# One scheduler for a whole kernel: pooled and local attention feeding a gated MLP

## The chip, the cores and the metric

The kernel runs on one core of one Trainium2 chip. The metric is the device time of one execution in microseconds (us). It has five kinds of worker: TensorE (PE in the profile, its weight loads PEld), VectorE (DVE), ScalarE (ACT), GpSimd (POOL) and the DMA queue that SyncE feeds (SP).

## The reference, cut to what matters

```python
def _attn_ref(q, k, v):                       # (8, 8, 576, 64) each
    q_d, k_d, v_d = (a.reshape(B, H, 144, 4, D).mean(axis=3) for a in (q, k, v))
    out_up = np.repeat(sm_attn(q_d, k_d, v_d), 4, axis=2)      # softmax attention on means of 4
    mask = np.abs(pos[:, None] - pos[None, :]) < 4
    scores = np.where(mask, scale * q @ k.T, -1e9)             # 7 neighbours at most
    return out_up + softmax(scores) @ v

def _moe_ref(x, w_gate, w_val, w_out):        # x (4608, 512), 512 -> 1536 -> 512
    return (sigmoid(x @ w_gate) * (x @ w_val)) @ w_out
```

The output of the attention, laid out by token, is the x of the MLP. All is float32 at the outside.

## The kernel before, in words

**Work.** Attention is done in 32 units of two heads: unit u is batch u // 4. The MLP is done in 9 chunks of 512 tokens (a batch has 576), each with 12 slices of the hidden width: a gate product (`pg`), a value product (`pv`), and an output product (`po`) that adds up in four PSUM banks. Numbers that need more than 16 bits are carried as a high and a low float16 part, so a product is three matmuls, and each tile is split twice: a high part by ACT and a low part by DVE or POOL.

**Three stretches.** First, batches 0 and 1 (units 0 to 7, function `early`, line 966), the loading and splitting of the weights (`wload`, `wmant`, `wshift`, `wjoin`, `wmax`, `whigh`, `wlow`, lines 210 to 252) and chunk 0 of the MLP. Second, chunk 1, while `combos` (line 736) forms the sums and differences of weight blocks from which the other chunks work with seven block products instead of eight, and writes them to DRAM. Third, chunks 2 to 8 by `pair` (line 816; its products are the matmuls at line 799), with the attention of batches 2 to 7 (units 8 to 31, function `later`, line 460) beside them.

**Operations of a unit.** `s` and `sd` are the local and the pooled scores on PE; `st`, `mx`, `sm`, `rc`, `dm`, `rd` are mask, maxima, sums and reciprocals on DVE; `ex`, `de` the exponentials on ACT; `sb`, `tm` subtract the maximum and multiply by the reciprocal, on POOL in `later` (line 507), and `tm` on DVE for batch 0 and on POOL for batch 1 in `early` (`divide`, line 1023); `pa`, `pb` add four q and k columns to one (lines 990, 995, and 624, 486 in `later`), `va`, `vB` the same for v (lines 1087, 1092, and 624, 575), all on POOL; `dn` normalizes the pooled weights; `tt`, `dt` are transposes, `do` and `x0`, `x1` the two products with v on PE; `oc` copies `do` out with the scale of the batch; `xa` adds both and `xh`, `xl` split the result (`xlow`, line 1130, on POOL).

**The scale of a batch.** v is scaled by a power of two that comes from a bound of its size over the batch: `vm` (function `vmax`, line 315) sums absolute values of one unit on ACT, `vs` brings the four units to one number over PE and DVE. For batch 0 `vm` reads `vd`, the tile that the pooled v is made from; for batches 1 and up it reads a tile of its own that `vload` (line 309) fetches, 320 KB per unit. In `early`, `do` waits for `vs` of its batch.

**Who sets the order.** Every operation has a name, an engine, an estimated duration and a list of operations that it must follow. There are two lists and two planners. `op` and `order` (line 1254) plan the first stretch; `op2` and `arrange` (line 1433) plan the rest. Both go forward in time and give a free engine the ready operation with the earliest latest start; `GOALS` (line 22) holds due times of the first list; `in_turn` is a hand-made order of PE for the second. `arrange` starts each engine where its work in the first list ends:

```python
free = {g: max([end[k] for k in seq if ops[k]["eng"] == g and k[:2] != "st"] + [0.0]) for g in engs}
```

At the end both plans are merged by planned start, and the instructions are issued in that order, engine by engine (line 1530). An engine works through its own instructions in order; between engines there are semaphores where data require them, and no others. Neither planner has an idea of one engine slowing another. Where PE is planned to be idle before chunk 0, `awake` (line 85) puts in matmuls whose results nobody reads.

**Memory.** `arena` holds staging tiles of the weights first and x of chunks 2 and up later, so a marker named `arena` stands before the second use: it follows the stores of chunk 0, its last `pv` and the joining of the output weights.

Of the kernel before, what the change touches and what calls it, by code (L numbers as in the profile page):

```python
# [21 lines left out]
GOALS = {'x0': 23.22, 'x0s': 8.14, 'pv': 48, 'pvs': 7.76, 'x1': 105.9, 'x1s': 18.75, 'po': 139.42, 'pos': 2.17}  # L22
# [37 lines left out]
GSCALE = 2.0 ** -17  # L60
# [10 lines left out]
def attention_moe(ctx, tc, qk, qkd, v, vd, wg, wv, wo, mask, out):  # L71
# [28 lines left out]
    head = part(40960, 2048).rearrange("p (h t) -> p h t", h=NPAIR)  # L100
    turns = {}
# [187 lines left out]
    def ratios(got):  # L289
# [9 lines left out]
        nc.vector.tensor_scalar(out=qmax, in0=qmax, scalar1=e, scalar2=2.0 ** -11, op0=ALU.mult, op1=ALU.mult)  # L299
# [15 lines left out]
    def vmax(u):  # L315
# [3 lines left out]
        src = vdraw[u].rearrange("p a b f -> p (a b f)") if u < NPAIR else vraw[u].rearrange("p a b -> p (a b)")  # L319
# [134 lines left out]
    work = {}  # L454

    def op2(name, eng, us, f, after=(), att=()):
        assert name not in work, name
        work[name] = dict(name=name, eng=eng, us=us, f=f, after=[a for a in after if a is not None], att=att)

    def later(u):  # L460
# [7 lines left out]
        def was(k, back):  # L468
            return f"{k}_{u - back}" if u - back >= NPLAIN else None
# [4 lines left out]
        def add(k, eng, us, f, after=(), att=()):  # L474
            op2(n(k), eng, us, f, [n(a) if a[-1] != "!" else a[:-1] for a in after if a is not None], [n(a) for a in att])
# [149 lines left out]

        add("qk", "D", 2.2, lambda: load_qk(u), [old("s", 2)])
        add("qkd", "D", 2.1, lambda: load_qkd(u), [old("pb", 1)])
        add("vd", "D", 1.4, lambda: load_vd(u), [old("vB", 1)])
        add("vw", "D", 1.2, lambda: vload(u), [old("vl1", NVR), f"x1{5 if u % NVR in (2, 3) else 7}!" if u < NPLAIN + NVR else None, "vm7!"])
# [5 lines left out]
        add("s", "E", 0.9, scores, ["qk", old("tt1", 3)], ["st0", "st1"])  # L635
        for par in range(2):
            add(f"st{par}", "V", 0.55, lambda par=par: masked(par), ["s"])
        add("mx", "V", 0.95, lambda: reduce("mx", ALU.max), ["st0", "st1"])
        add("sb", "P", 1.55, lambda: each_group("mx", ALU.subtract), ["mx"])
        add("ex", "A", 0.84, lambda: nc.scalar.activation(s["t"], s["t"], AF.Exp), ["sb"])  # L640
        add("sm", "V", 0.95, lambda: reduce("sm", ALU.add), ["ex"])
# [11 lines left out]
        for par in range(2):  # L653
            add(f"tt{par}", "E", 0.37, lambda par=par: turn(par), ["tm"], [f"tl{par}"])
            add(f"tc{par}", "A", 0.4, lambda par=par: turned(par, 0), [f"tt{par}", old("x1", 2)])
# [23 lines left out]
    def xsfree(c):  # L679
        return [f"g_{(c - 3) * (NFC // 2) - 1}_1_3"] if c >= 4 else ["pv1_11"] if c == 3 else ["head"]  # L680
# [932 lines left out]
```

## Time and profile before

| | us |
|---|---|
| median of three runs | 1021.35 (1018.09 to 1021.99) |
| the profiled execution | 1022.47 |
| its span, first to last instruction | 1020.3 |
| PE busy in it | 983.4 (96%), granted clock 0.975 on the mean |
| DVE, ACT, POOL busy in it | 644.5, 581.6, 375.9 |

What lies around the span is 2.2 us. A busy PE counts matmuls whose ends are modelled and which overlap, and the `awake` matmuls too, so idle time of PE is a lower bound of what the stretch loses.

### The profile page before, as it was taken

What the parts mean: (1) busy time and instruction counts of PE and PEld (TensorE: products, weight loads), DVE (VectorE), ACT (ScalarE), POOL (GpSimd) and SP (SyncE); (2) the same over time, 40 slices, a digit from 0 to 9 for tenths busy, and PEclk for the clock granted to TensorE, in tenths of its full rate; (3) what the DMA queues carried; (4) which work ended last, traced back from release to release, by engine and by line L of the source; (5) the groups of instructions that cost most, each with busy time, mean ns of one, the idle gap of its engine ahead of it and who ended that gap; (6) DMA issues with size and microseconds to landing.
All of it is one profiled execution on the core that took longest, in us unless ns stands there. A gap on an engine that the chain in (4) does not pass through costs nothing.

```text
span 1020.3 us, 21707 instructions
## 1 busy us (share of the span) xinstructions
PE 983.4 (96%) x8776; PEld 684.9 (67%) x8776; DVE 644.5 (63%) x1113; ACT 581.6 (57%) x1453; POOL 375.9 (37%) x374
## 2 busy tenths in 40 slices
PE   6978999999998999999999999999999999999998
PEld 4853455544545777777777777777777777777775
DVE  5789988478999665656566657565765445233223
ACT  4667765555464765676657565756565645334333
POOL 6442222367776446344523453445243303000000
PEclk7679999999999999999999999999999999999999
DMA  9886576845544755565545554654453335434431
GB/s 318 281 281 232 206 247 213 281 170 180 175 148 150 252 188 185 184 206 207 185 161 207 208 190 155 217 207 167 155 189 110 111 110 183 143 111 138 157 109 42
DMA packets 57700, 187.72 MB, mean 184 GB/s; under 512 B 15616, under 2 KB 19200, under 8 KB 57600
## 3 DMA queue, kind: packets, MB, share of 16 engines
q1 hardware_dynamic: 57600, 186.34, 52.8%
q8 instruction: 69, 1.13, 0.4%
q14 instruction: 31, 0.25, 0.1%
HBM read 165.87 MB, written 20.45 MB: 183 GB/s over the span
## 4 chain that ended last, share of the span: by engine, by line
PE 78%; DVE 12%; DMA 5%; issue 2%; ACT 2%; POOL 1%; SPq 0%; DVEq 0%; POOLq 0%; ACTq 0%
PE bank L799 37%; PE po L420 25%; PE x L420 3%; PE pg L420 3%; DVE arena L753 2%; PE od L420 2%; DMA qk<-in_qk_dram 2%; PE pv L420 2%; PE s L425 2%; PE sd L425 1%; PE at L545 1%; DVE arena L759 1%; PE adt L565 1%; DMA qkd<-in_qkd_dram 1%; DVE g L921 1%
## 5 line engine op out<-in xcount | busy, mean ns | idle before, releaser
L420 PE MATMUL po<-g,wo 128*128 128x512 f16 x1188 | 313.3, 382 | 0.0
L799 PE MATMUL bank<-arena,wg 128*128 128x256 f16 x1764 | 220.1, 273 | 0.0
L799 PE MATMUL bank<-arena,wv 128*128 128x256 f16 x1764 | 220.1, 273 | 0.0
L799 PEld LDWEIGHTS <-wg 128*128 128x128 f16 x1764 | 171.2, 98 | 47.6 <-issue 1.0
L799 PEld LDWEIGHTS <-wv 128*128 128x128 f16 x1764 | 170.4, 98 | 47.8
L420 PEld LDWEIGHTS <-wo 128*128 128x128 f16 x1296 | 124.7, 98 | 86.7 <-issue 6.6
L921 DVE SCALAR_TENSOR_TENSOR g<-wg,g 128x512 f16<-128x512 f32 x84 | 78.4, 933 | 34.9 <-ACT g L917 34.2
L846 ACT COPY bank<-wv 128x256 f32<-128x256 f32 x84 | 31.6, 377 | 98.4 <-DVE wg L844 63.6
L844 DVE TENSOR_TENSOR wg<-bank,wv 128x512 f32<-128x512 f32 x63 | 43.2, 686 | 59.9 <-PE bank L799 59.8
L839 ACT COPY wv<-bank 128x512 f32<-128x512 f32 x84 | 49.0, 584 | 51.4 <-PE bank L799 49.7
L420 PE MATMUL pg<-arena,wg 128*128 128x512 f16 x288 | 70.6, 395 | 7.2 <-POOL arena L1136 3.3
L420 PE MATMUL pv<-arena,wv 128*128 128x512 f16 x288 | 67.0, 383 | 0.0
L917 ACT ACTIVATE g<-wg 128x512 f16<-128x512 f32 x84 | 52.8, 629 | 22.7 <-DVE wg L827 22.7
L618 DVE TENSOR_TENSOR arena<-x,od 128x112 f32<-128x112 f32 (+12 forms) x72 | 21.6, 349 | 59.4 <-PE x L420 59.2
L728 POOL TENSOR_TENSOR arena<-arena 128x512 f16<-128x512 f32 (+1 forms) x35 | 41.4, 1189 | 46.8 <-ACT arena L724 46.8
L597 DVE SCALAR_TENSOR_TENSOR vblk<-vring,svb,vblk 64x640 f16<-64x640 f32 x48 | 51.8, 1080 | 9.6 <-ACT vblk L595 8.5
L420 PEld LDWEIGHTS <-wg 128*128 128x128 f16 x288 | 28.0, 101 | 42.6 <-issue 8.4
L844 DVE TENSOR_TENSOR wv<-bank,wv 128x512 f32<-128x512 f32 x21 | 14.4, 687 | 60.2 <-PE bank L799 60.2
L420 PEld LDWEIGHTS <-wv 128*128 128x128 f16 x288 | 28.0, 99 | 32.1 <-issue 1.9
L624 POOL TENSOR_TENSOR qkd<-qkd 128x576 f32<-128x576 f32 x24 | 29.9, 1246 | 53.0 <-DMA qkd<-in_qkd_dram 53.0
L841 ACT COPY wv<-bank 128x256 f32<-128x256 f32 x84 | 31.0, 369 | 30.1 <-PE bank L799 28.3
L535 POOL TENSOR_TENSOR ad<-e,sme 72x288 f32<-72x288 f32 x48 | 35.2, 750 | 34.7 <-PE adt L565 25.7
(182 smaller groups left out, 1640.5 us busy)
## 6 DMA issues: line engine op xcount, KB each, us to landing
wg<-wg SPq DMA_DIRECT2D x42, 896.0 KB, 4.6
wv<-wv SPq DMA_DIRECT2D x42, 896.0 KB, 4.6
qk<-in_qk_dram SPq DMA_DIRECT2D x30, 610.0 KB, 6.1
qkd<-in_qkd_dram SPq DMA_DIRECT2D x29, 576.0 KB, 3.8
arena<-in_wo_dram SPq DMA_DIRECT2D x24, 512.0 KB, 4.8
vd<-in_vd_dram SPq DMA_DIRECT2D x29, 384.0 KB, 3.7
vring<-in_v_dram SPq DMA_DIRECT2D x28, 320.0 KB, 5.2
out_dram<-arena SPq DMA_DIRECT2D x16, 512.0 KB, 5.2
```

What stands on the lines that cost most here:

```text
L420: nc.tensor.matmul(o, w[a], x[c], start=first and i == 0, stop=last and i == len(pairs) - 1)
L425: nc.tensor.matmul(o, w, x, start=True, stop=True)
L535: nc.gpsimd.tensor_tensor(out=AD[:, qb].rearrange("p c h k -> p h c k")[:, :, :, :KC], in0=s["e"][:, qb].rearrange("p h (c k) -> p h c k", ...
L597: nc.vector.scalar_tensor_tensor(out=VB[ps, 1, :, ps], in0=src, scalar=sc, in1=VB[ps, 0, :, ps], op0=ALU.mult, op1=ALU.subtract)
L728: eng.tensor_tensor(out=lo, in0=src, in1=hi, op=ALU.subtract)
L799: nc.tensor.matmul(o, w[:, a, k], x[:, xb, k, c], start=start and z == 0, stop=z == len(mms) - 1, skip_group_check=True)
L839: op2(f"sa_{n}_{i}", "A", 0.58, lambda i=i: nc.scalar.copy(snap(i)[:, HC:], banks[i]), [g(0), p("ad"), p("se")] + (["w1"] if n == 0 else []))
L841: op2(f"sb_{n}_{i}", "A", 0.37, lambda i=i: nc.scalar.copy(snap(i)[:, :HC], banks[i][:, RIGHT]), [g(1)])
L844: lambda i=i: nc.vector.tensor_tensor(out=vsum(n) if i else duo(n)[:, 1], in0=banks[i], in1=snap(i)[:, :CH], op=ALU.add),
L846: op2(f"se_{n}_{i}", "A", 0.38, lambda i=i: nc.scalar.copy(banks[i][:, LEFT], snap(i)[:, CH:]), [f"ad_{n}_{i}"])
L917: nc.scalar.activation(g[:, 0], tanh[c, fc], AF.Copy, scale=GSCALE)
L921: nc.vector.scalar_tensor_tensor(out=g[:, 1], in0=t, scalar=GSCALE, in1=g[:, 0], op0=ALU.mult, op1=ALU.subtract)
```

## The change

1. `op2`, `work` and `arrange` are gone: all operations go into one list `ops`, planned by one `order`. An engine may take work of the second and third stretch as soon as it is ready. PE chooses, by earliest latest start, among the first list and the next 14 operations of `in_turn`, whose due times count from a new goal `c1`. Dependencies that followed from the break between the lists are written out (`SAME`, `was`).
2. The planner has a lock: while a POOL operation or a DVE operation of the kinds in `TWO` is planned, no other such operation starts.
3. Some operations of `early` may go to either engine, and the planner chooses: `pb` (now with `pa` in it) and `vB` (now with `va` in it) as one or two reductions on DVE or as the additions on POOL; `tm` and `xl` on either.
4. For batch 1, `vm` reads `vd`, and its four `vload` transfers are gone. `do` no longer waits for `vs`; for batch 1 `oc` copies without the scale, and a new small ACT operation `or` scales in place once `vs` is there.
5. Estimated durations and goals are changed (a qk load 2.1 for 1.49, a weight tile 1.7 for 1.28, latency of a DMA 2.6 for 2.2).
6. The tiles of tanh, of g and of x of one unit lie in one fixed tile `spare`; slots in the weights' memory are packed closer; a power of two is moved from one scale (`GSCALE`) to another.

The core of the diff:

```diff
-GOALS = {'x0': 23.22, 'x0s': 8.14, 'pv': 48, 'pvs': 7.76, 'x1': 105.9, 'x1s': 18.75, 'po': 139.42, 'pos': 2.17}
+GOALS = {'x0': 22.36, 'x0s': 7.49, 'pv': 73.39, 'pvs': 6.2, 'x1': 99.09, 'x1s': 19.72, 'po': 150.09, 'pos': 1.17, 'c1': 159.4}
...
-        src = vdraw[u].rearrange("p a b f -> p (a b f)") if u < NPAIR else vraw[u].rearrange("p a b -> p (a b)")
+        src = vdraw[u].rearrange("p a b f -> p (a b f)") if u < NPLAIN else vraw[u].rearrange("p a b -> p (a b)")
...
+        def prep():
...
+            if chosen[n("pb")] == "V":
+                nc.vector.tensor_reduce(flat_, x, axis=AX.X, op=ALU.add)
+                return
+            nc.gpsimd.tensor_tensor(out=x[:, :, 0:2], in0=x[:, :, 0:2], in1=x[:, :, 2:4], op=ALU.add)
+            nc.gpsimd.tensor_tensor(out=flat_, in0=x[:, :, 0], in1=x[:, :, 1], op=ALU.add)
...
+            if chosen[n("vB")] == "V":
+                for ps in HALVES:
+                    nc.vector.tensor_reduce(VDB[ps, :, ps], vdraw[u][ps], axis=AX.X, op=ALU.add)
+                return
...
-            nc.scalar.activation(s["od"], s["do"][:, :SD], AF.Copy, scale=sxb[:, b : b + 1])
+            nc.scalar.activation(s["od"], s["do"][:, :SD], AF.Copy, scale=sxb[:, b : b + 1] if first else 1.0)
+
+        def dscale():
+            nc.scalar.activation(s["od"], s["od"], AF.Copy, scale=sxb[:, b : b + 1])
...
-        unit_op("pa", "P", 1.3, prep_a, ["qkd"])
-        unit_op("pb", "P", 0.85, prep_b, ["pa"], new=[("qks", "qks_")], use=["qkd_"])
+        unit_op("pb", "V", 1.27, prep, ["qkd"], new=[("qks", "qks_")], use=["qkd_"], alt=("P", 2.1))
...
-        unit_op("tm", "V" if first else "P", 0.95 if first else 1.7, divide, ["rc"], use=["t_"])
+        unit_op("tm", "V", 0.95, divide, ["rc"], use=["t_"], alt=("P", 1.6))
...
-        unit_op("va", "P", 1.05, vda, ["vd"] + ["vm"] * first)
-        unit_op("vB", "P", 1.3, vdb, ["va"], new=[(f"vdb{u % 2}", "vdb_")], use=["vd_"])
-        unit_op("do", "E", 0.8, dout, ["dc", "vB", f"vs{b}!"], new=[("bank", "do_"), ("od", "od_")], use=["adt_", "vdb_"])
+        unit_op("vB", "V", 1.75, vdb, ["vd", "vm"], new=[(f"vdb{u % 2}", "vdb_")], use=["vd_"], alt=("P", 2.35))
+        unit_op("do", "E", 0.8, dout, ["dc", "vB"], new=[("bank", "do_"), ("od", "od_")], use=["adt_", "vdb_"])
...
-        unit_op("xl", "P", 1.6, xlow, ["xh"], use=["xs_"])
+        unit_op("xl", "P", 1.6, xlow, ["xh"], use=["xs_"], alt=("V", 0.85))
...
+    TWO = ("jn", "lo", "sh", "tm", "gl", "vl", "m", "p1", "p2", "cs", "cl", "t0", "t3", "t4", "t5", "t6", "t9", "ot", "ol", "a1", "xl")
+    two = lambda k, x: x == "P" or x == "V" and (k.startswith(TWO) and not k.startswith(("mx", "ml")) or k[:3] == "r1_")
...
+                for x in ENGS:
...
+                    for l, k in choices:
+                        if ops[k]["ways"][x][1] and port > now + 1e-9:
+                            continue
+                        got = places(ops[k], now) if ops[k]["new"] else []
+                        if got is not None:
+                            break
...
+                    if ops[k]["ways"][x][1]:
+                        port = end[k]
...
-    run = sorted([(start[k], i, k, ops[k]["f"]) for i, k in enumerate(seq)] + [(when[k], len(seq) + i, k, work[k]["f"]) for i, k in enumerate(turn_)])
     with tc.manual_schedule(engines={E.PE, E.DVE, E.Activation, E.Pool, E.SP}):
-        for _, _, k, f in run:
+        for k in seq:
             if k in spare:
                 awake(spare[k][1], spare[k][0])
-            f()
+            ops[k]["f"]()
```

`ENGS` is "NEVAPD": at one moment of the plan PE is asked first, then DVE, ACT, POOL, the DMA queue. The lock is a rule of the plan; the program that is issued has the same kinds of semaphores as before.

## Rows read from the trace of the kernel before

**Rows 1.** The page: span of the profiled execution.
```profile
span 1020.3 us, 21707 instructions
```

**Rows 2.** Windows: busy us of PE, PEld, DVE, ACT, POOL; PEclk, DMA share, GB/s.
```profile
0.00:17.00 17.00, 9.97 (x100) 6.61 (x100) 8.92 (x16) 8.40 (x21) 10.58 (x19) 0.90 0.91 317
17.00:66.00 49.00, 42.57 (x517) 36.38 (x517) 35.37 (x75) 30.32 (x96) 22.70 (x30) 0.69 0.94 295
66.00:125.00 59.00, 51.19 (x229) 22.78 (x229) 55.06 (x110) 43.17 (x102) 14.43 (x12) 0.91 0.63 221
125.00:198.00 73.00, 71.84 (x503) 41.73 (x503) 55.55 (x104) 41.80 (x93) 16.76 (x18) 1.00 0.71 245
198.00:334.00 136.00, 125.49 (x974) 66.12 (x972) 121.38 (x186) 72.58 (x177) 96.52 (x76) 0.97 0.49 170
334.00:860.00 526.00, 525.93 (x5307) 398.26 (x5306) 321.96 (x555) 325.87 (x845) 214.93 (x222) 1.00 0.51 180
860.00:1020.30 160.30, 156.40 (x1158) 112.98 (x1155) 46.21 (x69) 59.44 (x123) 0.00 (x0) 1.00 0.35 120
```

**Rows 3.** Windows of the awake matmuls alone: PE busy, PEclk, DMA share, GB/s.
```profile
17.00:66.00 49.00, 4.53 (x22) 0.69 0.94 295
```

**Rows 4.** Waits of PE from 17 to 66: us in total, times, longest.
```profile
PE s L1008 <- DMA qk<-in_qk_dram: 4.6, 2, 2.9
```

**Rows 5.** Waits of PE from 66 to 125.
```profile
PE pg L420 <- POOL arena L1136: 3.3, 1, 3.3
PE pg L420 <- ACT wg L248: 2.5, 2, 1.8
PE pg L420 <- DVE wg L252: 1.4, 2, 1.2
```

**Rows 6.** Waits of PE from 198 to 334, the two longest.
```profile
PE sd L425 <- DVE pvb L176: 2.1, 1, 2.1
PE mxt L165 <- DVE mxr L158: 1.9, 1, 1.9
```

**Rows 7.** DVE groups from 198 to 334: busy us, mean ns, idle before.
```profile
L753 DVE TENSOR_TENSOR arena<-arena 128x256 f32<-128x256 f32 x48 | 35.6, 781 | 1.9 <-POOL arena L748 1.3
L759 DVE TENSOR_TENSOR arena<-arena 128x1024 f16<-128x1024 f32 x12 | 18.8, 1563 | 0.4 <-ACT arena L756 0.3
L921 DVE SCALAR_TENSOR_TENSOR g<-tanh,g 128x512 f16<-128x512 f32 x12 | 14.0, 1165 | 1.2 <-ACT g L917 1.2
```

**Rows 8.** Timeline of DVE, two short instances: start us, us.
```profile
291.80 1.71 DVE L753 TENSOR_TENSOR arena<-arena 128x256 f32<-128x256 f32 x4
...
298.88 1.21 DVE L759 TENSOR_TENSOR arena<-arena 128x1024 f16<-128x1024 f32 x1
```

**Rows 9.** DVE groups from 860 to the end, where POOL is idle.
```profile
L921 DVE SCALAR_TENSOR_TENSOR g<-wg,g 128x512 f16<-128x512 f32 x22 | 15.2, 691 | 15.6 <-ACT g L917 15.6
```

**Rows 10.** Timeline of POOL, 214 to 222: start us, us.
```profile
214.94 1.47 POOL L507 TENSOR_TENSOR t<-t,sm 128x768 f32<-128x768 f32 x1
216.37 1.33 POOL L624 TENSOR_TENSOR qkd<-qkd 128x576 f32<-128x576 f32 x1
217.66 1.65 POOL L507 TENSOR_TENSOR t<-t,mx 128x768 f32<-128x768 f32 x1
219.27 1.00 POOL L624 TENSOR_TENSOR vd<-vd 128x384 f32<-128x384 f32 x1
```

**Rows 11.** Timeline of DVE in the same stretch.
```profile
215.02 5.54 DVE L753 TENSOR_TENSOR arena<-arena 128x256 f32<-128x256 f32 x4 [1.27 <-POOL arena L748]
```

**Rows 12.** POOL groups from 125 to 198: the lines of later.
```profile
L624 POOL TENSOR_TENSOR qkd<-qkd 128x576 f32<-128x576 f32 x1 | 1.2, 1151 | 0.0
L486 POOL TENSOR_TENSOR qks<-qkd 128x288 f32<-128x288 f32 x1 | 0.7, 712 | 0.1
```

**Rows 13.** DVE groups from 0 to 420: a reduction of 768 elements.
```profile
L504 DVE TENSOR_REDUCE mx<-t 128x12 f32<-128x768 f32 x9 | 8.5, 948 | 0.2
```

**Rows 14.** Timeline of PE: unit 4 transposed, scale of batch 1, its product.
```profile
97.15 0.59 PE L1079 MATMUL adt<-ident,ad 72*128 72x72 f32 x6
...
121.78 0.38 PE L266 MATMUL mxt<-ident,mxr 1*128 1x1 f32 x2
...
124.69 0.90 PE L420 MATMUL od<-adt,vdblk 128*128 128x144 f32 x6
```

**Rows 15.** The line of vload: issues by form, first and last start.
```profile
L311 SPq DMA_DIRECT2D vring<-in_v_dram x4: 327/328/422, 38.3 to 101.7; - x4
```

More of the change, by code (lines that the diff above doesn't have):

```diff
@@ L452, in pooled_pairs @@
                 for qb in range(2) for h in range(2)]
[L454 to L458, printed above, removed]
+    SAME = dict(s="s{}", pb="pb{}", sd="sd{}", vB="vB{}", tt0="tt0_{}", tt1="tt1_{}", dn1="dn{}", dt="dt{}", do="do{}", x1="x1{}", xa1="xa1{}", qk="qk{}", tc0="tc0_{}", oc="oc{}", mx="mx1_{}", sm="sm{}")
     def later(u):
@@ L474, in add @@
         def add(k, eng, us, f, after=(), att=()):
-            op2(n(k), eng, us, f, [n(a) if a[-1] != "!" else a[:-1] for a in after if a is not None], [n(a) for a in att])
+            op(n(k), eng, us, f, [n(a) if a[-1] != "!" else a[:-1] for a in after if a is not None], att=[n(a) for a in att])
         def old(k, back):
@@ L953, in attention_moe, with op, engine @@
     ops = {}
-    def op(name, eng, us, f, after=(), new=(), use=(), by=None):
+    freed = {}
+    def op(name, eng, us, f, after=(), new=(), use=(), att=(), alt=None):
         assert name not in ops, name
-        ops[name] = dict(name=name, eng=eng, us=us, f=f, after=list(after), new=list(new), use=list(use), by=by)
+        ops[name] = dict(name=name, eng=eng, us=us, f=f, after=[a for a in after if a is not None], new=list(new), use=list(use), alt=alt)
+        for z, x in enumerate(att):
+            ops[name]["new"].append((["att"], f"{name}.{z}"))
+            freed[f"{name}.{z}"] = x
+    chosen = {}
+    def engine(name):
+        return nc.vector if chosen[name] == "V" else nc.gpsimd
     where = {}
@@ L1023, in divide @@
         def divide():
-            eng = nc.vector if first else nc.gpsimd
-            eng.tensor_tensor(out=groups(), in0=groups(), in1=s["sm"].unsqueeze(2).to_broadcast([P, 4 * NH, WIN]), op=ALU.mult)
+            engine(n("tm")).tensor_tensor(out=groups(), in0=groups(), in1=s["sm"].unsqueeze(2).to_broadcast([P, 4 * NH, WIN]), op=ALU.mult)
         def turn(par):
@@ L1525, in attention_moe @@
-    turn_, when, fin = arrange()
+    CAPS = dict(qk=2, qkd=1, vd=1, vt0=1, vt1=1, vt2=1, vt3=1, qks=1, t=3, at=2, e=1, ad=1, adt=1, vdb0=1, vdb1=1, od=2, xs=1, stage=NST, wa=2,
+                tanh=2, g16=3, att=2, gate=1, val=1, o0=1, o1=1, o2=1, o3=1)
+    LAT = dict(D=2.6, E=0.3, V=0.12, A=0.12, P=0.15, N=0.0)
+    EXTRA, AHEAD = 0.5, 14
+    ENGS = "NEVAPD"
+    import heapq
+    after = {k: [] for k in ops}
+    users = {}
+    for o in ops.values():
+        o["after"] = list(dict.fromkeys(o["after"]))
+        for a in o["after"]:
+            after[a].append(o["name"])
+        for key in o["use"]:
+            users.setdefault(key, []).append(o["name"])
+        for _, key in o["new"]:
+            users.setdefault(key, []).append(o["name"])
+            if key in freed:
+                users[key].append(freed[key])
```

548 lines of the change are left out of this document (245 added, 303 removed).

## The prediction

> **What bounds the kernel now.** I read the page first and then cut the span into the kernel's own stretches [rows 1, 2]. From 334 us on PE is idle for 0.1 of 526 us and for 3.9 of the last 160.3 us: there TensorE is the bound, and no order of the other engines gives anything back. All that can be won lies before 334. The first 17 us are the start (PE idle 7.0). I call the next four stretches A (17 to 66, attention of batch 0), B (66 to 125, the first gate and value products), C (125 to 198, the rest of chunk 0 with batch 1) and D (198 to 334, chunk 1 with the weight combinations).
>
> In A PE is idle for 49 − 42.6 = 6.4 us, and another 4.5 us of its busy time are fillers [rows 3]; its granted clock is 0.69 on the mean, between the levels of 1.2 and 2.4 GHz, and the DMA engines are 94% busy: this stretch waits for loads, and the longest wait of PE is for a qk tile, 4.6 us [rows 4]. In B PE is idle for 7.8 us while DVE is busy for 55.1 of 59: the split weights come late (2.5 + 1.4 us), and once the low part of x from POOL does (3.3 us) [rows 5]. In C PE is idle for 1.2 us only; DVE is idle for 73 − 55.6 = 17.4 us and POOL for 56. In D PE is idle for 10.5 us, DVE is busy for 121.4 of 136 and POOL for 96.5; the longest waits of PE are for small DVE results that stood in DVE's queue behind longer work [rows 6].
>
> DVE in D is busier than its work. The difference of two weight blocks takes 781 ns on the mean and 1.71 / 4 = 0.43 us in a short instance; the low part of a combination takes 1563 ns against 1.21 us [rows 7, 8]; the low part of g takes 1165 ns against 691 where POOL is idle [rows 7, 9]. Where the two engines meet, four block differences take 5.54 us while four POOL instructions run back to back at 1.0 to 1.65 us each: DVE gets through about one per POOL instruction [rows 10, 11]. Over D that is 48 × 0.35 + 12 × 0.35 + 12 × 0.47 = 16.8 + 4.2 + 5.7 = 27 us of DVE's 121.
>
> **The change part by part.** Sums are made against the profiled execution, 1022.5 us; the median of the runs is 1.1 us less, and about 0.5% (5 us) is what a measurement of this kernel tells from no change.
>
> *One list.* The break between the lists keeps DVE and POOL from the attention of units 8 and up during C: POOL does one pooled q and k sum of such a unit there, nothing else of it [rows 12]. With one list, the front of units 8 to 11 (mask, maxima, sums, normalizing) can run in C in the 17.4 us of DVE and 56 us of POOL that are idle. It needs no `arena`; only the results of the units do. What leaves D makes room there. Every unit moved takes its qk, qkd and vd loads along, over an SP queue whose engines are 71% busy in C: room for some 73 × 0.29 = 21 us of transfers. The weight combinations can't move: they stand behind the marker `arena`, at the end of chunk 0. For D's idle 10.5 us the ends are 0 (D is bound by other things) and 10.5 − about 0.5 (C, where DVE has room, idles 1.2 of 73). I take 9, nearest to C, since more than 15 us leave DVE's queue in D, by moving or by fewer meetings with POOL.
>
> *The lock in the plan.* It adds no wait on the chip. It changes who stands in which order, so that a one-operand DVE instruction rather than a block difference is in turn while POOL works. Its ends are 0 and the 27 us of DVE above, off PE's path but for D; it is in the 9 above. In B DVE's meetings with POOL are few (POOL is busy 14.4 of 59), so nothing is taken for it there.
>
> *Either engine.* `xl` on DVE (estimated by the change at 0.85 against 1.6 us) can remove the 3.3 us wait in B. The other choices put work on DVE: a reduction of 768 elements is 948 ns [rows 13], so by elements the q and k sum (1152) is an estimated 1.4 us and the v sum (two halves of 768) 1.9 us, 3.3 per unit. In A DVE has 13.6 us idle, in B 3.9. I take it that the sums of batch 0 go to DVE in A, beside the loads, at no cost, and those of batch 1 mostly stay on POOL. For B I take 4 of the 7.8 us: the 3.3, and 0.7 of the waits for weights, which stay since DVE is full.
>
> *Loads.* A takes 49 us at 295 GB/s, 14.5 MB, while by their shapes the four units of batch 0 need 4 × 1.89 = 7.6 MB and the first gate and value slice 1 MB: weights are loaded ahead of what PE waits for. Dearer loads in the plan and the due time of `pv0` moved from 48 to 73.39 put weights later. Of the 6.4 + 4.5 us I take 5, about the wait for qk [rows 4]; the ends are 0 and 10.9. The price is that weights come later into B, where DVE is the bound; it is in the small gain for B.
>
> *Clock.* A and B ran at 0.69 and 0.91. If PE's own work in A (42.6 − 4.5 = 38.1 us) ran at full clock, 38.1 × 0.31 = 11.8 us would go, in B 51.2 × 0.09 = 4.6. A denser A brings some of it; I take 3, nearer to the lower end since A stays tied to loads.
>
> *Bound of v from vd.* Four transfers of 320 KB are gone [rows 15]: at 295 GB/s 4.4 us of the queue, one of them in A, three in B and just before, where the DMA engines are 63% busy; nothing of it ended a wait of PE, so 0. The transposes that `do` of unit 4 needs were done at 97.7 and it ran at 124.7, after the scale of batch 1 at 121.8 [rows 14]; without that wait four such products of 0.9 us move from C into idle time of B at best, which is less than 1 us of PE time in all since the final product still waits for the scale; counted 0. What is late next is the scale itself: it now needs the last vd tile of batch 1, which has one buffer and stands behind `vB` of unit 6. C has nothing else that waits for it before x of units 4 to 7, and PE has 12 output products there to put in between. Added: four `or` and longer `vm`, on ACT, idle for 40% of these stretches: 0.
>
> *Memory and constants* change no amount of work: 0; new false dependencies by the shared tile would cost, but `arena` is used in the same way now.
>
> Sum: 9 (D) + 4 (B) + 5 (A) + 3 (clock) = 21 us; 1022.5 − 21 = 1001.5, less the 1.1 of the median: **1000 us**.
>
> **The rivals.**
>
> *1. The plan's lock does not reach the chip.* No semaphore keeps the engines apart, the plan drifts against the chip within some us, and DVE meets POOL in D as often as now. For it: the qk wait and the low clock show how much a plan of this kernel can be off in A. Then D gains only by what moved into C, some 2 of the 9: 1000 + 7 = 1007.
>
> *2. D is full of a resource that reordering cannot empty.* If a POOL instruction and a DVE instruction with two operands in SBUF take strict turns, D holds 96.5 us of POOL (with some waits of its own in it), 48 × 0.43 = 20.6, 12 × 1.21 = 14.5 and 12 × 0.69 = 8.3 us of DVE: 140 us in a stretch of 136. Avoiding meetings then only makes one engine wait in the plan rather than on the chip; D gains nothing, A stays at 94% of the DMA engines and B at 93% of DVE, and the 3.3 us for `xl` are all: 1021.35 − 3.3 = 1018. The Trainium skill, SBUF — State Buffer, section "Who interferes with whom", states this as a rule: the pair of ports that the two share is an exclusive lock, a DVE instruction with two SBUF inputs contends with a GpSimd instruction that reads SBUF, the later one blocks fully, and on trn2 a tensor_reduce never contends. The 5.54 us of four block differences agree [rows 10, 11], and no row here shows a reduction that was held up. Against the rival speaks C: the front of units 8 to 11 carries POOL work out of D, for which C has 56 idle us.
>
> *3. DVE, already the bound of B, gets the pooled sums.* The plan asks DVE before POOL, and with a string of two-operand instructions (splits of weights) each follows the other at once, so POOL never finds the lock open and DVE ends up with the sums of both batches: 8 × 3.3 = 26.4 us. A's and B's idle DVE time is 13.6 + 3.9 = 17.5, of which perhaps three quarters fit, 13; the other 13 us delay the split weights and so PE in B: 1021.35 + 13 = 1034, with none of the gain in D to set against it if POOL's later work is starved in the same way. It decides from the point where more than some 17.5 / 1.65 = 10 of the 16 sums run on DVE between 17 and 125.
>
> **How the numbers follow.** Forecast 0.58 (1000); rival 1, 0.14 (1007); rival 2, 0.11 (1018); rival 3, 0.17 (1034). Faster by over 0.5% is below 1016.2: 0.58 + 0.14 = 0.72; the same 0.11; slower 0.17. The low end is all of A, B and D's idle time and fillers (10.9 + 7.8 + 10.5 = 29.2) with all of the clock (16.4): 1021.4 − 45.6 = 976. The high end takes in rival 2 and part of rival 3: 1027. Outside I leave about 0.08 below and 0.1 above. The forecast's own range is 985 to 1012.
>
> **What would show it.** Right: in D PE idle for 3 us or less, block differences near 0.5 us on the mean, and instructions of the masked scores (line of `masked`) on DVE before chunk 1 begins; `pg` of the first slice at 60 rather than 66; PE idle for 4 in B. From the first matmul of the third stretch to the end the time should stay as it is, 686 us, less what attention moved ahead of it. Wrong: `tensor_reduce` of pooled sums in numbers on DVE in B with PE waiting for DVE's low parts (rival 3); POOL and DVE together still over the length of D (rival 2); or new waits of PE in the third stretch, which I count as nothing.

## The result, and the profile after

The changed kernel takes 1003.96 us in the median of 4 runs (1001.01 to 1006.42), the kernel before 1019.72 us on the same chip; the ratio is 0.9848 with an interval of 0.9803 to 0.9892. A second measurement on another occasion gave 1003.84 us and 0.9845 (0.982 to 0.9871). The forecast was 1000 us in a range of 976 to 1027: the direction is right and the size is 4 us off. Its terms were not, though: some came twice as large, some not at all, some with the other sign, and that they cancel to 4 us is luck.

The page of the changed kernel, against [rows 1]:

```profile
span 1004.6 us, 21808 instructions
...
PE 976.5 (97%) x8800; PEld 682.8 (68%) x8800; DVE 621.8 (62%) x1123; ACT 584.1 (58%) x1457; POOL 344.9 (34%) x361
```

To see where the time went, both traces are cut at the same events rather than at the same times: the first gate product (`pg`), the first one of chunk 1, and the first bank product of the third stretch. The windows of the kernel before (columns as in [rows 2]):

```profile
17.00:66.31 49.31, 42.88 (x519) 36.69 (x520) 35.52 (x76) 30.64 (x97) 23.01 (x30) 0.69 0.94 294
66.31:197.63 131.32, 122.34 (x726) 63.99 (x725) 110.09 (x213) 84.32 (x193) 30.51 (x30) 0.96 0.67 234
197.63:326.14 128.51, 119.00 (x923) 60.96 (x918) 114.45 (x175) 69.24 (x165) 94.75 (x74) 0.97 0.49 168
326.14:1020.30 694.16, 689.18 (x6519) 516.61 (x6517) 375.47 (x636) 388.99 (x979) 217.07 (x224) 1.00 0.48 166
```

And of the changed kernel:

```profile
17.00:56.06 39.06, 33.14 (x461) 28.41 (x462) 34.91 (x76) 30.91 (x97) 13.66 (x16) 0.88 0.91 294
56.06:191.51 135.45, 126.92 (x840) 67.87 (x835) 120.17 (x234) 90.31 (x213) 43.85 (x46) 0.95 0.77 261
191.51:301.66 110.15, 108.95 (x841) 56.76 (x839) 84.44 (x153) 59.13 (x140) 62.83 (x50) 1.00 0.42 152
301.66:1004.60 702.94, 694.99 (x6540) 520.75 (x6536) 370.05 (x643) 393.92 (x985) 216.23 (x234) 0.99 0.48 167
```

The first gate product comes 10.2 us earlier, the stretch behind it is 4.1 us longer, chunk 1 is 18.4 us shorter, and the rest is 8.8 us longer: −10.2 + 4.1 − 18.4 + 8.8 = −15.7 us, the difference of the spans. (This profiled execution took 1006.42 us, 2.5 over the median. In the second measurement's, with a span of 1000.4 us, chunk 1 takes 110.1 us and the rest 700.5, so that the last term lies between 6.3 and 8.8 us.)

In chunk 1 TensorE's idle time went from 9.5 to 1.2 us. The groups of DVE there (window 191 to 320) answer to [rows 7]:

```profile
L758 DVE TENSOR_TENSOR arena<-arena 128x256 f32<-128x256 f32 x48 | 21.3, 483 | 1.0
L764 DVE TENSOR_TENSOR arena<-arena 128x1024 f16<-128x1024 f32 x12 | 16.2, 1346 | 0.0
L928 DVE SCALAR_TENSOR_TENSOR spare<-spare 128x512 f16<-128x512 f32 x12 | 10.2, 849 | 2.2 <-ACT spare L924 2.2
```

Block differences fell from 781 to 483 ns, low parts of combinations from 1563 to 1346, low parts of g from 1165 to 849: 14.3 + 2.6 + 3.8 = 20.7 of the 27 us of stretch are gone. The front of later units does run ahead of chunk 1, which no row of before shows; DVE, 119 to 191.5, mask and maxima:

```profile
L500 DVE SCALAR_TENSOR_TENSOR t<-s,mk 128x384 f32<-128x384 f32 x4 | 2.1, 536 | 1.0 <-PE s L431 1.0
L509 DVE TENSOR_REDUCE mx<-t 128x12 f32<-128x768 f32 x2 | 1.9, 952 | 0.1
```

Behind the first gate product the 3.3 us wait for `xl` of [rows 5] is gone, but others stand in its place. PE's waits from 62 to 155, the three longest:

```profile
PE s L1026 <- DMA qk<-in_qk_dram: 2.5, 1, 2.5
PE at L1051 <- POOL t L1042: 2.0, 1, 2.0
PE pv L426 <- DVE wv L258: 0.9, 1, 0.9
```

They cost more than their length. PE's timeline (start us, us), the next gate product behind the first wait (three short groups of matmuls lie between), an undisturbed one, and the one behind the other two:

```profile
73.56 4.90 PE L426 MATMUL pg<-arena,wg 128*128 128x512 f16 x12
78.30 2.75 PE L426 MATMUL pv<-arena,wv 128*128 128x512 f16 x12
...
89.11 4.45 PE L426 MATMUL pv<-arena,wv 128*128 128x512 f16 x10 [0.90 <-DVE wv L258]
```

Twelve matmuls take 4.90 us behind a wait of 2.52 us and 2.75 us otherwise; ten take 4.45 behind the other two, where 2.3 is usual. The granted clock from 60 to 100 is 0.83 on the mean, between its levels of 1.2 and 2.4 GHz. (In the second measurement's trace the two products took 4.22 and 3.18 us.)

In the third stretch the groups of PE show what was moved there; the output products from the first bank product on, of before and of after:

```profile
L420 PE MATMUL po<-g,wo 128*128 128x512 f16 x1009 | 269.1, 379 | 0.0
```

```profile
L426 PE MATMUL po<-spare,wo 128*128 128x512 f16 x1020 | 272.3, 379 | 1.0 <-DVE spare L928 1.0
L804 PE MATMUL bank<-arena,wg 128*128 128x256 f16 x1764 | 222.0, 274 | 2.3 <-ACT wv L843 2.3
```

Eleven matmuls of chunk 1's last output product now lie behind the first bank product (3.2 us), and two new waits, 2.3 us for the first snapshot and 1.0 us for a low part of g, stand at the start. The granted clock of the first 22 us of this stretch is 0.84 (0.92 in the second measurement), against 1.00 before, so matmuls behind these waits take longer too.

### The profile page after: what moved, and what is told of

It reads as the page before. It is cut to its first block, busy times and chain, and to the rows that moved or that the text cites. A ratio compares the mean times of both kernels' runs of the same rounds, so it can differ in the third digit from the quotient of the medians.

```text
span 1004.6 us, 21808 instructions
## 1 busy us (share of the span) xinstructions
PE 976.5 (97%) x8800; PEld 682.8 (68%) x8800; DVE 621.8 (62%) x1123; ACT 584.1 (58%) x1457; POOL 344.9 (34%) x361
## 4 chain that ended last, share of the span: by engine, by line
PE 88%; DVE 5%; DMA 4%; ACT 2%; issue 1%; SPq 1%; POOL 0%; DVEq 0%; ACTq 0%
PE bank L804 38%; PE po L426 27%; PE pg L426 5%; PE pv L426 5%; PE x L426 3%; DMA qk<-in_qk_dram 2%; PE s L431 2%; PE od L426 2%; PE sd L431 2%; PE at L550 1%; DMA wo<-in_qk_dram 1%; PE adt L570 1%; DVE spare L928 1%; DMA arena<-in_wv_dram 0%; DVE arena L733 0%
## 5 line engine op out<-in xcount | busy, mean ns | idle before, releaser
L426 PE MATMUL po<-spare,wo 128*128 128x512 f16 x1188 | 310.7, 379 | 1.0 <-DVE spare L928 1.0
L426 PEld LDWEIGHTS <-wo 128*128 128x128 f16 x1296 | 122.1, 98 | 86.4 <-issue 3.5
L848 DVE TENSOR_TENSOR wg<-bank,wv 128x512 f32<-128x512 f32 x63 | 43.4, 690 | 97.4 <-PE bank L804 92.4
L928 DVE SCALAR_TENSOR_TENSOR spare<-wg,spare 128x512 f16<-128x512 f32 x84 | 67.1, 799 | 18.2 <-ACT spare L924 18.1
L924 ACT ACTIVATE spare<-wg 128x512 f16<-128x512 f32 x84 | 52.9, 630 | 33.2 <-DVE wg L831 32.9
L848 DVE TENSOR_TENSOR wv<-bank,wv 128x512 f32<-128x512 f32 x21 | 14.5, 691 | 88.7 <-PE bank L804 88.7
L733 POOL TENSOR_TENSOR arena<-arena 128x512 f16<-128x512 f32 (+1 forms) x35 | 35.7, 1030 | 71.6 <-ACT arena L729 71.4
L817 ACT ACTIVATE wg<-bank,tsc 128x128 f32<-128x128 f32 (+6 forms) x78 | 34.2, 485 | 39.4 <-PE bank L804 39.3
L602 DVE SCALAR_TENSOR_TENSOR vblk<-vring,svb,vblk 64x640 f16<-64x640 f32 x48 | 47.7, 994 | 1.1
L512 POOL TENSOR_TENSOR t<-t,sm 128x768 f32<-128x768 f32 x24 | 37.1, 1544 | 31.9 <-DVE sm L518 31.8
```

The costliest lines, as they stand in the source:

```text
L426: nc.tensor.matmul(o, w[a], x[c], start=first and i == 0, stop=last and i == len(pairs) - 1)
L512: nc.gpsimd.tensor_tensor(out=groups(), in0=groups(), in1=s[k].unsqueeze(2).to_broadcast([P, 4 * NH, WIN]), op=op_)
L602: nc.vector.scalar_tensor_tensor(out=VB[ps, 1, :, ps], in0=src, scalar=sc, in1=VB[ps, 0, :, ps], op0=ALU.mult, op1=ALU.subtract)
L733: eng.tensor_tensor(out=lo, in0=src, in1=hi, op=ALU.subtract)
L817: nc.scalar.activation(t[:, o : o + w], src[:, o : o + w], AF.Tanh, scale=tsc[:, b, fc : fc + 1])
L848: lambda i=i: nc.vector.tensor_tensor(out=vsum(n) if i else duo(n)[:, 1], in0=banks[i], in1=snap(i)[:, :CH], op=ALU.add),
```

## The experiments

In all of them "the change" is the changed kernel at 1003.9 us, and every ratio is to the kernel before. Where a list's content changes, its best due times change too. In runs 2 to 5, 7 and 8 they (in 5 also the planner's margin, in 7 its margin and look-ahead) were set anew by a search over the list's own schedule; run 12 has those of run 8, the others those of their base. The differences below are of medians from different occasions; by the ratios (difference to 0.9847, times 1020 us) they come out smaller: 5, 9.5, 6.4, 5.7 and 3.4 us for runs 1, 2, 3, 5 and 7.

**1. The lock alone taken out.**

```
-    two = lambda k, x: x == "P" or x == "V" and (k.startswith(TWO) and ...
+    two = lambda k, x: False
```

> The changed kernel with one line altered: no operation holds the lock in the plan, so GpSimd and two-operand VectorE work are planned side by side again; one list, either engine and the bound from vd stay, goals too. Theory (the lock in the plan is what takes the meetings out of chunk 1): block differences back from 0.48 to 0.7 us or more on the mean, the stretch from the first product of chunk 1 to the first of the third stretch back from 110 to 120 us or more, 1012 us. Rival (one list and moved work carry the gain): block differences slower, but PE covers it, 1004 to 1006. A third way (the lock makes VectorE wait in the plan for nothing): faster than 1004.

Measured: 1010.82 us, 0.9896 (0.9875 to 0.9916), 7 us slower than the change. The first bank product comes at 313.7, 12 us later, though chunk 1 began 3.6 us earlier; PE idles for 8.0 of its 125.8 us. The first gate product comes at 50.0, 6 us earlier than in the change, and the rest behind the first bank product takes 695.4 us instead of 702.9, so that about half of what chunk 1 loses comes back there. DVE's group, 150 to 345:

```profile
L758 DVE TENSOR_TENSOR arena<-arena 128x256 f32<-128x256 f32 x48 | 27.1, 604 | 0.7
```

So the plan's lock does reach the chip without any semaphore: 483 ns with it, 604 without. But 604 is also well under 781: one list and the choice of engine thin out the meetings by themselves. The due times here are those found for the list with the lock; how much of the 7 us a search for this list would take back was not tried.

**2. One list taken out** (nothing of the second list is placed on an engine before the first list's last operation on it).

```
+    first_list = set(ops)
...
+                        if x != "N" and k not in first_list and of_first[x]:
+                            continue
```

> The changed kernel with the break between the lists put back: an engine takes no operation of the second list before it has planned its last one of the first; goals searched again for this rule. Theory (front of units 8 to 11 in C is worth some us): no masked scores of units 8 and up on VectorE before the last product of chunk 0, 1008 us (4 slower than the change). Rival (one list is most of the gain): 1014 or more. The other side (C is bound by PE and D is relieved by the lock alone): 1004.

Measured: 1015.39 us, 0.994 (0.9919 to 0.9962), 11.5 us slower. Chunk 1 begins at 189.1, 2.4 us earlier than in the change, and takes 120.9 us instead of 110.2; the rest takes 703.7. The break costs about the 9 us that the forecast gave D, and it costs them in chunk 1.

**3. The choice of engine taken out** (pooled sums and `xl` on GpSimd; the division on VectorE in batch 0 and GpSimd in batch 1).

```
-        unit_op("pb", "V", 1.27, prep, ["qkd"], new=[("qks", "qks_")], use=["qkd_"], alt=("P", 2.1))
+        unit_op("pb", "P", 2.1, prep, ["qkd"], new=[("qks", "qks_")], use=["qkd_"])
...
```

> The changed kernel with the four operations of batches 0 and 1 fixed to the engines they had before (pooled sums and low part of x on GpSimd, division on VectorE for batch 0); goals searched again. Theory of the prediction (the low part of x on VectorE is worth 3.3 us in B): 1007. Rival (choice is worth nothing once the order is planned well): 1003 to 1005. Other side (VectorE is better off without the sums): below 1002.

Measured: 1013.02 us, 0.9909 (0.9887 to 0.993), 9 us slower. The first gate product comes at 62.4 instead of 56.1, the first bank product at 308.7 instead of 301.7. The three parts taken out singly cost 7 + 11.5 + 9 = 27.5 us (5 + 9.5 + 6.4 = 21 by the ratios), more than the 16 that they bring together: none of them is worth a fixed sum.

**4. The bound of batch 1's v from its own tile again, first try.** The output of this list differs from the reference's (relative error 0.154), and why is not known; its edit is that of run 5, so its time is given, with that reserve.

```
-        src = vdraw[u].rearrange(...) if u < NPLAIN else vraw[u].rearrange(...)
+        src = vdraw[u].rearrange(...) if u < NPAIR else vraw[u].rearrange(...)
...
-        unit_op("do", "E", 0.8, dout, ["dc", "vB"], ...
+        unit_op("do", "E", 0.8, dout, ["dc", "vB", f"vs{b}!"], ...
```

> The changed kernel with the bound of batch 1 from a tile of its own again: four more transfers of 320 KB, the product waits for the scale, no rescaling; goals searched again. Prediction: counted as nothing, 1004. Rival (four transfers in a stretch that waits for loads cost their 4.4 us): 1008, with PE waiting longer for qk tiles between 17 and 75 us. Other side (the scale comes later with vd than with a tile of its own): 1000.

Measured: 1018.62 us, 0.9985 (0.9969 to 1.0002), nearly all of the gain gone, where the forecast had priced this part at 0. The first gate product comes at 62.8.

**5. The same edit with other due times.**

```
-GOALS = {'x0': 19.99, 'x0s': 8.52, 'pv': 74.63, ... 'x1': 100.18, ... 'c1': 171.08}
+GOALS = {'x0': 19.29, 'x0s': 6.72, 'pv': 73.21, ... 'x1': 81.76, ... 'c1': 172.1}
...
-    EXTRA, AHEAD = 0.5, 14
+    EXTRA, AHEAD = 0.63, 14
```

> The changed kernel with part 4 undone as a whole, as in the run before it of this kind, but with other due times: the bound of batch 1's v comes from its own tile of v again (four more loads of 320 KB, the output product of the dense part waits for the scale, no rescale afterwards). If part 4 is worth nothing by itself, as forecast, and the earlier run's 1018.6 us lay in its due times (first gate product at 62.8, 6.7 us later than in the change, and a chunk 1 that began 10.5 us later), this list should come within about 5 us of the changed kernel: 1001 to 1010 us, chunk 1 beginning by 195. If the loads or the wait for the scale cost several us whatever the due times, 1013 us or more, with the loss between 17 and 200.

Measured: 1009.62 us, 0.9902 (0.9869 to 0.9936). Nine us of run 4 were its due times and the planner's margin. Some 6 us against the change stay (the intervals of 0.9869 to 0.9936 and 0.982 to 0.9871 meet at their ends). Chunk 1 itself takes 108.9 us, less than in the change; the first gate product comes at 59.3, against 56.1 and 54.9 in the two traces of the change.

**6. The lock alone put into the kernel before** (in the second planner; lists, engines and due times as before; each output product is also made to follow the one before it in its bank).

```
...
+                if g in "VP" and two(k):
+                    port = t + work[k]["us"]
```

> The kernel before with the lock alone: two lists, engines as before, all due times as before, but the second planner never lets a VectorE operation with two operands lie beside a GpSimd operation. My theory (the lock pays only because one list and the choice of engine make room for it, VectorE being busy 121 of 136 us in chunk 1): block differences fall from 0.78 us on average to about 0.5, but VectorE and GpSimd wait for each other, so that the first bank product comes at most 4 us earlier or even later: 1014 to 1024 us. Rival (the lock by itself is the gain, as the meetings stretched 27 us of VectorE's work): the first bank product by 316, 1010 us or less.

Measured: 1025.87 us, 1.0055 (1.0036 to 1.0075): 0.55%, or 5.6 us, slower than the kernel without it. The block differences did get short (DVE, 100 to 345), the low parts of the combinations did not (1855 ns, 1563 before), and chunk 1 takes 128.0 us, against 128.5:

```profile
L759 DVE TENSOR_TENSOR arena<-arena 128x1024 f16<-128x1024 f32 x12 | 22.3, 1855 | 4.6 <-ACT arena L756 4.5
L753 DVE TENSOR_TENSOR arena<-arena 128x256 f32<-128x256 f32 x48 | 22.0, 499 | 1.0
```

One wait of PE took the place of the meetings, at the end of chunk 1:

```profile
PE po L420 <- DVE g L924: 9.0, 1, 9.0
PE mxt L165 <- DVE mxr L158: 2.8, 1, 2.8
```

DVE's timeline shows what stood ahead of that low part of g (L924):

```profile
315.99 1.22 DVE L759 TENSOR_TENSOR arena<-arena 128x1024 f16<-128x1024 f32 x1
317.31 1.56 DVE L753 TENSOR_TENSOR arena<-arena 128x256 f32<-128x256 f32 x4
318.78 3.21 DVE L728 TENSOR_TENSOR arena<-arena 128x512 f16<-128x512 f32 x2
321.92 1.64 DVE L924 SCALAR_TENSOR_TENSOR g<-tanh,g 128x512 f16<-128x512 f32 x1
```

The work that the lock pushes back doesn't vanish; with chunk 1's load unchanged it piles up ahead of the third stretch, and the first short result that TensorE needs stands behind it. The loss itself lies elsewhere: of the 8.0 us by which this execution's span is longer (1028.3, against 1020.3; it is the slowest of its nine), 2.5 lie ahead of chunk 1 and 6.0 in the third stretch (700.2 us, against 694.2), whose start has a new wait of PE:

```profile
PE s L425 <- ACT e L529: 4.2, 2, 3.8
```

What puts that wait there was not followed further. The timeline above also shows a meeting: four block differences take 1.56 us while GpSimd is idle, two splits 3.21 us beside a GpSimd combination, where one that began ahead of such a combination took 0.69 (at 307.21). The Trainium skill, SBUF — State Buffer, section "Who interferes with whom", has it that the later instruction of such a pair blocks fully; the trace agrees as far as 4 differences at 1.56 us with GpSimd idle and 5.54 us beside it [rows 11]; what is blocked there is each difference by about one GpSimd instruction, not all four by one.

**7. Only the four loads put back** (bound of batch 1 from its own tile; the product of the dense part still ahead of the scale).

```
+            unit_op("vw", "D", 1.1, lambda: vload(u), new=[("vw", "vw_")])
+            unit_op("vm", "A", 0.92, lambda: vmax(u), ["vw"], use=["vw_"])
...
```

> The changed kernel with only the four loads of part 4 put back: the bound of batch 1's v from its own tile, and vd's conversion in batch 1 waits no longer for the bound; the output product still runs ahead of the scale. Due times set anew. If four transfers of 320 KB cost only queue time that other work hides (forecast: 4.4 us of queue, 0 on the path): 1000 to 1008 us. If the queue is the limit up to chunk 1, each transfer delays the rest by its 1.1 us: 1007 to 1012 us, with idle time of PE before 190 about 4 us above the changed kernel's.

Measured: 1009.88 us, 0.988 (0.9851 to 0.991), the same as run 5. So the freed product brings nothing that can be measured; with the loads back, and the due times found, runs 5 and 7 are 3 to 6 us slower than the change; that is less than due times and margin moved between runs 4 and 5, and the interval of this run overlaps with the change's. PE's idle time from 17 to 190 is 16.0 us, against 14.5 and 15.3 in the two traces of the change, not 4 more. What can be seen is that the loads hold up the queue. The waits of the SP queue, 17 to 190, at the line that loads v: first before, then run 5, then this run.

```profile
SPq L311 <- ACT junk L322: 4.1, 3, 2.0
```

```profile
SPq L317 <- ACT junk L328: 7.2, 2, 6.3
```

```profile
SPq L317 <- ACT junk L328: 5.1, 3, 3.7
```

Each load of a v tile waits until ACT has read the one before it for the bound, and all later loads wait behind it. The change has no such row. But all waits of the queue from 17 to 190 add up to 110.1 us in run 5, 107.6 here, and 109.0 and 108.5 in the change: the queue stands still elsewhere there, and these rows do not show that they are the loss. Here the first gate product comes at 59.7 instead of 56.1, as in run 5; why is open.

**8. The weight sums on either engine.**

```
-            nc.gpsimd.tensor_tensor(out=f, in0=w[:, 2 * j : 2 * j + 2, 0], ...
+            engine(f"cf_{i}").tensor_tensor(out=f, in0=w[:, 2 * j : 2 * j + 2, 0], ...
...
-        op(f"cf_{i}", "P", 2.1, whole_, back("cs") if i else ["pv11"])
+        op(f"cf_{i}", "P", 2.1, whole_, back("cs") if i else ["pv11"], alt=("V", 1.25))
...
```

> The changed kernel with the twelve weight sums that were bound to GpSimd free to go to either engine, under the same lock, with due times set anew. My theory: the last of these sums releases the first snapshot of the third stretch (2.3 us of PE idle there, the stall of 7.2 us in the first 40 us of that stretch against 2.1 before) and holds GpSimd in chunk 1; freed, the stall in the first 40 us of the third stretch falls to 4 us or less and chunk 1 begins earlier: 996 to 1002 us. Rival: VectorE is the scarcer of the two in chunk 1, and each sum that it takes delays block differences by about 1.25 us; nothing is gained: 1003 to 1010 us.

Measured: 1004.05 us, 0.9832 (0.9807 to 0.9858), the same as the change. The wait for the first snapshot is gone, PE idles for 0.5 of the first 40 us of the third stretch instead of 3.7, and the rest behind the first bank product takes 696.3 us instead of 702.9 (700.5 in run 9). But the first gate product comes at 60.8, 4.7 us later, with one long wait ahead of it (PE, 17 to 62):

```profile
PE sd L431 <- POOL qks L1014: 5.5, 1, 5.5
```

Chunk 1's first gate product comes at 180.0, 11.5 us earlier, only because 72 matmuls of chunk 0's output products (16 us) now stand behind it, the first 36 of them here:

```profile
182.55 7.93 PE L426 MATMUL po<-wo 128*128 128x512 f16 x36
```

Without them the 127.7 us from there to the first bank product are 111.5, against 110.2. The meetings are longer (DVE, 150 to 345):

```profile
L758 DVE TENSOR_TENSOR arena<-arena 128x256 f32<-128x256 f32 x48 | 26.7, 598 | 1.0
```

So the third stretch did gain what the theory said, and the start of the list lost about as much. Whether one comes from the other, or the later start only from the due times that were found, this run does not show.

**9. The change once more**, beside the last three.

> The changed kernel itself, once more, beside the three runs that follow, so that they are compared with it on one chip: 1000 to 1007 us, ratio 0.98 to 0.989.

Measured: 1003.84 us, 0.9845 (0.982 to 0.9871).

**10. Fillers in the waits behind the first gate product.**

```
-            if prev is not None and start[k] < start["pg0"] and start[k] - end[prev] > 0.8:
+            if prev is not None and start[k] < start["po0"] and start[k] - end[prev] > 0.8:
```

> The changed kernel with fillers also in the four waits of 0.8 us and over that its list holds between the first gate product and the first output product: 3, 3, 1 and 6 matmuls of 0.27 us (3.5 us in all), in waits that PE has anyway. In the changed kernel 12 gate matmuls took 4.90 us behind the 2.52 us wait at 70.42, and 10 value matmuls 4.45 us behind the waits at 87.23 and 89.11, where 2.75 us for 12 is usual: 2.2 and 2.2 us given to a clock of 0.83 in 60 to 100. Theory that the waits let the clock fall and that short fillers prevent it: the clock from 60 to 100 rises above 0.9 and the kernel gains 2 to 5 us on the change. Rival (the clock goes by more than these waits, or 13 fillers are too few): clock within 0.05 of the change's, the time equal within 2 us.

Measured: 1000.40 us, 0.9813 (0.9788 to 0.9837).

**11. Three times as many in the same waits.**

```
-  spare[k] = (tag, int((start[k] - end[prev] - 0.4) / 0.29))
+  spare[k] = (tag, int((start[k] - end[prev] - 0.4) / 0.29) * (3 if start[k] > start["pg0"] else 1))
```

> As the run with fillers, with three times as many in the same four waits: 9, 9, 3 and 18 matmuls (10.5 us of PE time at 0.27 us). Where the waits are as long as in the changed kernel (2.5, 0.2, 0.4 and 2.0 us) some of it lies on PE's path. If the clock is what the stretch is short of: the clock from 60 to 100 at 0.95 or more and a gain of 0 to 4 us on the change, the fillers' own time taking back the rest; if not, a loss of 3 to 6 us on the change.

Measured: 999.96 us, 0.9813 (0.9784 to 0.9842). The windows from 60 to 100 of run 9, of run 10 and of this run:

```profile
60.00:100.00 40.00, 33.34 (x195) 16.46 (x193) 37.53 (x81) 33.02 (x78) 12.57 (x15) 0.87 0.87 294
```

```profile
60.00:100.00 40.00, 33.43 (x210) 17.11 (x208) 37.59 (x78) 31.08 (x75) 11.26 (x16) 0.91 0.87 286
```

```profile
60.00:100.00 40.00, 35.79 (x240) 19.65 (x239) 37.91 (x81) 32.63 (x79) 12.66 (x15) 0.96 0.88 291
```

The clock rises with the fillers, 0.87, 0.91, 0.96 (0.83 in the first profile of the change), and the product behind the qk wait takes 4.22, 3.44 and 3.08 us. The same product in runs 10 and 11:

```profile
77.06 3.44 PE L426 MATMUL pg<-arena,wg 128*128 128x512 f16 x12
```

```profile
75.01 3.08 PE L426 MATMUL pg<-arena,wg 128*128 128x512 f16 x12
```

But behind the qk wait the fillers stand after the wait, not in it, and take time themselves. Run 10:

```profile
72.87 1.56 PE L1026 MATMUL s<-qk 64*64 64x64 f32 x48 [3.07 <-DMA qk<-in_qk_dram]
74.36 0.82 PE L88 MATMUL awake<-idle 128*128 128x256 bf16 x3
```

From the end of that wait to the end of the product it is 8.0 us in the first trace of the change, 7.9 in run 9, 7.6 in run 10 and 7.3 in run 11: most of what the product gains went into the fillers. The clearer case is the wait for the division, where they do stand in the wait. The ten value matmuls behind it took 4.45 and 3.18 us in the change; in runs 10 and 11 they take the usual time:

```profile
91.15 2.33 PE L426 MATMUL pv<-arena,wv 128*128 128x512 f16 x10 [0.90 <-DVE wv L258]
```

```profile
88.76 2.33 PE L426 MATMUL pv<-arena,wv 128*128 128x512 f16 x10 [0.90 <-DVE wv L258]
```

That cheap matmuls in a wait keep the clock up behind it is shown there, with one trace for each run; the mean clock of run 10 differs from run 9's by no more than the two traces of the change do. That the kernel gains by it is not quite shown: 3.4 and 3.9 us in the medians, with intervals that overlap. From the first gate product to chunk 1, where the fillers are, the traces of runs 10 and 11 take 135.0 and 133.8 us, against 135.5 and 134.9 in the change, so 1.6 us of the gain at most is seen in its place.

**12. Weight sums and fillers together.**

> The changed kernel with the weight sums on either engine and short fillers until the first output product (15 waits, 7 of them behind the first gate product, 0.3 to 1.2 us each). The run with the sums alone gave 1004.0 us with the same clock of 0.83 in 80 to 100 and a wait of 5.5 us at 17 to 60. If both help: 996 to 1002 us; if the fillers do nothing, 1001 to 1006 us.

Measured: 1004.05 us, 0.9849 (0.982 to 0.9878): no better than the change.

## Why the prediction was right, and where it was not

**D, 9 us:** the idle time was right, 9.5 to 1.2 us, and by the mechanism named (less DVE work in chunk 1 and fewer meetings). (The prediction's D, 198 to 334, holds 7.9 us of the third stretch, which began at 326.1; what it calls the 686 us of that stretch are 694.2.) The length fell twice as much, 18.4 us, because work left the stretch and the clock rose from 0.97 to 1.00: PE's busy time fell by 10.0 us. Some 3 us of that (the eleven output matmuls) reappear in the third stretch, and the scores of later units ahead of chunk 1. Experiments 1, 2 and 6 divide the term: without one list the lock leaves chunk 1 as long as it was (128.0 us) and the kernel 5.6 us slower; without the lock one list keeps chunk 1 at 125.8 us; with the lock and the choice of engine but two lists it takes 120.9.

**A, 5 us, and the clock, 3:** the first gate product comes 10.2 us earlier, more than their sum, but not by the step named. A's idle time hardly fell, from 6.4 to 5.9 us: the waits for qk of 4.6 us [rows 4] became 2.5, and small waits for DVE and ACT filled the rest (PE of the change, 17 to 56):

```profile
PE s L1026 <- DMA qk<-in_qk_dram: 1.8, 2, 1.3
PE at L1051 <- DVE t L1035: 1.6, 1, 1.6
PE x L426 <- ACT wg L228: 1.5, 1, 1.5
PE s L1026 <- DMA wo<-in_qk_dram: 0.7, 1, 0.7
```

What fell is PE's busy time, 42.9 to 33.1 us: the clock went from 0.69 to 0.88, which the term of 3 us had far too low (39 × 0.19 = 7 us), and some score products moved behind the first gate product (198 matmuls of `s` between it and chunk 1 instead of 96, 54 of them out of chunk 1). The new plan also puts 81 `awake` matmuls ahead of the first gate product instead of 57. How much of the higher clock is theirs and how much the denser order's, no run separates.

**B, 4 us:** failed. The wait for `xl` went, as forecast, but the stretch from the first gate product to chunk 1 grew by 4.1 us. PE's idle time in it stayed, 9.0 and 8.5 us, and its busy time grew by 4.6, as scores and transposes that moved in take some 5 us more. The step that B's waits would shorten by 4 missed what takes their place: a stretch that begins 10 us earlier meets loads that don't, so a qk wait of 2.5 us stands in it, and the plan's choice put a division on GpSimd that PE then waited 2.0 us for. The clock was low behind them, 2.2 us twice; the kernel before has slow products behind its own waits there too.

**Bound of v from vd, 0:** too low, as far as the runs go. Experiments 5 and 7 put it at 3 to 6 us with the due times that were found, with the loss ahead of the first gate product (59.3 and 59.7, against 56.1 and 54.9). The step counted the loads by their bytes and by PE's waits. It did not read SP's own waits, where the kernel before stands still for the bound's buffer (4.1 us, 3 times); but since the queue's waits add up to the same with and without these loads, that this is the cause is not shown. That the freed product and the `or` are worth nothing fits (1009.62 against 1009.88 us). That due times and the planner's margin alone can move such a list by 9 us (runs 4 and 5) limits what can be said.

**Third stretch, 0:** failed, +6.3 to 8.8 us: a moved product, two waits at its start and a lower clock behind them. The prediction named new waits there as what would show it wrong. In experiment 8, with the weight sums free, this stretch is 6.6 us shorter, but the first gate product comes 4.7 us later and the time is the same.

**The rivals.** Rival 1 (the plan's lock does not reach the chip) falls by 483 against 604 ns, and by 499 against 781 in experiment 6. Rival 2 (D full of the shared port) falls too, for this list: PE idles for 1.2 us, since POOL's share of chunk 1 went from 94.8 to 62.8 us, 13 us of that into the stretch ahead of it (30.5 to 43.9). By the rival's own sum, POOL's time and DVE's at its short times, chunk 1 now holds 62.8 + 43.4 = 106 us in 110, so it is nearly full again. The sign that the prediction named for this rival, POOL and DVE together over the length of D, was too loose: they are busy for 84.4 + 62.8 = 147 us there. In experiment 6, where work could not leave the stretch, D gains nothing, as the rival says. The prediction's chances do not fit its range: it gives rival 3, at 1034 us, 0.17 and what lies above 1027 about 0.1. Rival 3 (the pooled sums on DVE) did not come: between 17 and 125 one sum of v runs on DVE, of 16, and two of q and k before 17:

```profile
L1106 DVE TENSOR_REDUCE vdblk<-wv 64x192 f32<-64x768 f32 x2 | 1.9, 944 | 0.0
L1011 DVE TENSOR_REDUCE qks<-wo 128x288 f32<-128x1152 f32 x1 | 1.4, 1354 | 1.4 <-DMA wo<-in_qkd_dram 1.4
L1011 DVE TENSOR_REDUCE qks<-qkd 128x288 f32<-128x1152 f32 x1 | 1.4, 1352 | 0.0
```

The estimates of 1.4 and 1.9 us for these were right; that DVE would end up with the sums was not: as the plan is written, whichever of the two is free first takes the work, and between 17 and 125 that was mostly GpSimd.

## What to carry to other kernels

A rule for the order (never A beside B) is worth what the list lets it move: the same rule lost 5.6 us in the old order and was worth 5 to 7 us in the new one (each with the due times of its base), so price it together with the room that it needs, and follow every instruction that it pushes back to the place where it lands. Before a row of waits is called the cause, add up all waits of that engine or queue in both kernels, and before a stretch is called longer, count the same work in it. And to measure one part of a planned kernel by undoing it, set the plan's due times anew; here they and the planner's margin made 9 us, more than some of the parts.

## What the runs showed of the hardware

The size of the clock's loss behind short waits was not expected: after 2.5 us of waiting, 12 matmuls that need 2.75 us took 4.90, so that the wait cost nearly as much again behind it; and 10 matmuls behind a wait of 2.0 us and a shorter one took 4.45 and 3.18 us in two traces, and the usual 2.33 once 6 or 18 fillers stood in the first. And the order of instructions alone, with the same engines and no semaphore between the two, was enough to shorten a VectorE operation by 36% (781 to 499 ns in experiment 6).
